# Pooled value rows inside block 0's value tiles, and a new order of the prologue: attention with pooled keys, then a gated MLP, on one core

## The chip, the core and the metric

The kernel runs on one core of a Trainium2 chip. The metric is the device time of one execution in microseconds (us). Three runs of the kernel before gave 698.35, 698.39 and 698.47, so its time is **698.39 us** (the median).

## What is computed

```python
def _attn_ref(q, k, v):                       # (4, 8, 768, 64) each, float32
    ...
    block, window = (32, 16)
    nb = S // block                           # 24
    k_sum = k.reshape(B, H, nb, block, D).max(axis=3)
    v_sum = v.reshape(B, H, nb, block, D).mean(axis=3)
    scores_l = scale * np.matmul(q, k.transpose(0, 1, 3, 2))
    mask_l = np.abs(pos[:, None] - pos[None, :]) < window
    scores_s = scale * np.einsum('bhsd,bhnd->bhsn', q, k_sum)
    scores_s = scores_s + np.log(block)
    ...  # masked scores_l and scores_s side by side, softmax over both: a
    v_all = np.concatenate([v, v_sum], axis=2)
    return np.matmul(a, v_all)

def _moe_ref(x, w_gate, w_val, w_out):        # x: the attention's output, 3072 x 512
    g = x @ w_gate                            # 512 x 1536
    silu = g * (1.0 / (1.0 + np.exp(-g)))
    return silu * (x @ w_val) @ w_out         # 1536 x 512
```

Every query thus sees 31 neighbouring keys and 24 pooled ones (a maximum over 32 keys for the scores, a mean over 32 rows for the values). The three weight matrices arrive as float64 and are turned into float32 on the chip.

## The kernel before

**Tiles.** The 3072 tokens are worked on as six blocks (k = 0 to 5) of 512. In a block the attention goes by head pairs (u = 0 to 3: two heads of 64 are the 128 partitions), the MLP by twelve weight tiles (j = 0 to 11, 128 of the 1536 hidden units each). 64 queries meet 96 keys at once (the window and its margins), and the 24 pooled keys stand behind them: a row of 120 scores (KC = 120, KW = 96).

**Steps of a head pair.** Scores on TensorE (`scores`; in block 0 apart as `sw` for the windows and `sp` for the pooled keys), row maxima on VectorE (`ttr0`, `ttr1`, L414), exponentials on ScalarE (`exp0`, `exp1`, L428), reciprocals of the sums on VectorE (`rcp`, L445 and L446), the scaling by them (`nrm`, L450), transposes on TensorE into PSUM (`tr0`, `tr1`, L465), their copies to SBUF (`pt0`, `pt1`, L162 or L164), the value products on TensorE (`out`, L492), and from PSUM the high and the low part of the result in the type fp32r (`split` makes xh, `rest` makes xl), which are the MLP's input. `zeros` (L598) issues filler matmuls on a tile of zeros; a digit behind a step's engine letter asks for so many columns of 128 of them ahead of the step.

**Steps of a weight tile.** A load on SyncE (`w_load`, raw_*), the magnitude on ScalarE (`w_abs`, L187, m_*), four integer steps on VectorE (`w_c1` L192, `w_c2` L196, `w_s1` L204, `w_s2` L211; the last two read two tensors), then the high part (`w_hi`, L162) and the low part (`w_lo`, L158) of w_*. g and v of tile 0 are handled apart, those of the other tiles together (gv); o is the output matrix. Then `gate` and `val` (L527: three products for each of four head pairs on 512 columns), `silu` (L533), `mul` (L538), `ah` and `al` (high and low part), and `down` (L577).

**The value tiles of block 0.** They lie in one SBUF tile, vrows, in three loads: vE (`ve`) the even value tiles and the matrix of means, vR (`vr`) the end of the even ones, vO (`vo`) the odd ones. `fv` (v_sums, L341) makes the block means of all values on TensorE, and `fvc` (v_keep) copies them to rows 96 to 119 of vs. For block 0 (OWN = (0,)) the value products contract over the 96 window rows alone (a_out, L492), and the 24 pooled rows are added by products of their own, `outp` (a_out_pooled, L500), two per head pair. In the later blocks a_values (L321 and the copy behind it) writes the pooled rows under the windows' values, and one product contracts over all 120 rows. A function v_copy that does the same for vrows (step `spc`) is there and unused.

**What sets the order.** The text PROLOGUE holds block 0's attention and MLP, block 1's attention, and the decoding of all weights. One word is one step; `=` and letters behind it choose its engine (a ScalarE, d VectorE, p GpSimd), its PSUM bank (g, y or c) and its fillers. The words are issued in the order of the text, and a chain of order dependencies (`after`) keeps that order on each engine, SyncE's queue of loads too. Behind it a loop runs blocks 1 to 5's MLP with the attention of blocks 2 to 5 put in at fixed places; the change leaves that loop alone. `after` takes no wait away: a step also waits for its data and for the buffers that it writes.

## Time and profile before

| | |
|---|---|
| median of three runs | 698.39 us |
| profiled execution, its own time | 698.23 us |
| span of its instructions | 696.4 us |
| TensorE (PE) busy | 687.0 us, 99% of the span, 4540 matmuls |
| weight loads (PEld), beside the matmuls | 558.0 us, 80% |
| VectorE (DVE) busy | 263.4 us, 38% |
| ScalarE (ACT) busy | 295.1 us, 42% |
| GpSimd (POOL) busy | 144.4 us, 21% |
| mean granted clock of TensorE | 0.999 of full speed |
| loads and stores over the span | 62.04 MB, 89 GB/s |

The span begins with the first instruction and ends with the last; the profiled execution's own time is 1.8 us longer. A share of busy time is a mean over the whole span: the page's 40 slices of 17.4 us show VectorE at six tenths or more in the first eight and at four or less in all later ones, and the transfers at seven tenths or more in the first five alone, while TensorE is at nine tenths or more from the third slice on, but for the last. A time in a row below is counted from the span's start.

### The profile page before, as it was taken

How to read it: one execution, taken by the hardware profiler on the slowest of the kernel's cores; microseconds unless marked ns; L12 is line 12 of the kernel's file. 1: busy time of each engine (PE TensorE's matmuls, PEld its weight loads, DVE VectorE, ACT ScalarE, POOL GpSimd, SP SyncE). 2: the span in 40 equal slices, each digit the busy share in tenths (PEclk: the TensorE clock that was granted, in tenths of full speed). 3: DMA queues.
4: the chain of work that ended last, by engine and by line, in shares of the span. 5: the costliest groups of instructions: out<-in, count | busy, mean ns of one | idle time of the engine just before them, and what ended most of it. 6: DMA issues, size and time to landing. Idle time of an engine off the chain costs nothing.

```text
span 696.4 us, 11370 instructions
## 1 busy us (share of the span) xinstructions
PE 687.0 (99%) x4540; PEld 558.0 (80%) x4540; DVE 263.4 (38%) x749; ACT 295.1 (42%) x707; POOL 144.4 (21%) x122
## 2 busy tenths in 40 slices
...
GB/s 341 325 323 294 274 72 133 85 155 118 84 62 0 62 56 88 84 26 58 107 24 144 74 56 61 3 60 61 61 62 53 8 24 1 61 1 0 1 0 61
DMA packets 52676, 62.04 MB, mean 89 GB/s; under 512 B 23152, under 2 KB 40944, under 8 KB 51088
## 3 DMA queue, kind: packets, MB, share of 16 engines
q1 hardware_dynamic: 52624, 61.32, 27.4%
q8 instruction: 36, 0.59, 0.4%
...
## 4 chain that ended last, share of the span: by engine, by line
PE 95%; DMA 3%; ACT 1%; DVE 0%; SPq 0%; issue 0%; DVEq 0%; ACTq 0%
PE g L527 29%; PE v L527 28%; PE acc L577 27%; PE xo L492 4%; PE sc L371 3%; PE pp L465 3%; DMA vrows<-in_vE 2%; DMA consts<-in_consts 1%; PE xo L500 1%; ACT p L428 0%; DVE w_gv L158 0%; DMA out<-o 0%; PE pp L598 0%; PE pv L341 0%; PE pv L320 0%; ACT L428 0%
## 5 line engine op out<-in xcount | busy, mean ns | idle before, releaser
L577 PE MATMUL acc<-w_o,ah 128*128 128x512 f32 x576 | 178.1, 390 | 0.0
L538 DVE TENSOR_TENSOR a<-v,a 128x512 f32<-128x512 f32 x72 | 49.6, 690 | 295.9 <-PE v L527 268.5
L527 PE MATMUL g<-xh,w_gv 128*128 128x512 f32 x480 | 160.3, 395 | 0.6 <-DVE w_gv L158 0.6
L527 PE MATMUL v<-xh,w_gv 128*128 128x512 f32 x480 | 158.2, 390 | 0.0
L158 POOL TENSOR_TENSOR al<-a,ah 128x512 fp32r<-128x512 f32 x63 | 81.5, 1294 | 322.0 <-ACT ah L162 322.0
L577 PEld LDWEIGHTS acc<-w_o,ah 128*128 128x128 f32 x576 | 108.2, 188 | 22.7
L577 PE MATMUL acc<-w_o,al 128*128 128x512 f32 x288 | 114.2, 397 | 0.0
L533 ACT ACTIVATE a<-g 128x512 f32<-128x512 f32 x72 | 43.1, 599 | 165.8 <-PE g L527 165.6
L527 PEld LDWEIGHTS g<-xh,w_gv 128*128 128x128 f32 x480 | 90.1, 188 | 23.0 <-issue 1.9
L527 PEld LDWEIGHTS v<-xh,w_gv 128*128 128x128 f32 x480 | 90.1, 188 | 18.8 <-issue 0.2
L162 ACT CAST ah<-a 128x512 fp32r<-128x512 f32 x72 | 44.7, 620 | 136.4 <-DVE a L538 136.3
L527 PE MATMUL g<-xl,w_gv 128*128 128x512 f32 x240 | 93.6, 390 | 0.0
L527 PE MATMUL v<-xl,w_gv 128*128 128x512 f32 x240 | 93.4, 389 | 0.0
L428 ACT ACTIVATE p<-p,nm 128x120 f32<-128x120 f32 x192 | 73.1, 382 | 5.7 <-DVE nm L414 5.5
L577 PEld LDWEIGHTS acc<-w_o,al 128*128 128x128 f32 x288 | 54.1, 188 | 10.8
L450 POOL TENSOR_TENSOR p<-p,ri 128x960 f32<-128x960 f32 x21 | 38.1, 1815 | 99.1 <-DVE ri L446 79.4
L527 PEld LDWEIGHTS v<-xl,w_gv 128*128 128x128 f32 x240 | 45.1, 188 | 9.2
L527 PEld LDWEIGHTS g<-xl,w_gv 128*128 128x128 f32 x240 | 45.1, 188 | 8.7
L414 DVE CUSTOM_DVE_ANT_0 p<-sc,consts 128x120 f32<-128x120 f32 x192 | 40.8, 277 | 3.5 <-PE sc L371 3.5
L428 ACT ACTIVATION_READ_ACCUMULATOR p<-p,nm 128x1 f32 x192 | 35.9, 187 | 0.0
L162 ACT CAST xh<-xo 128x512 fp32r<-128x512 f32 x24 | 13.9, 591 | 46.8 <-PE xo L492 46.8
L527 PE MATMUL g<-xh,w_g 128*128 128x512 f32 x96 | 32.9, 401 | 0.0
...
## 6 DMA issues: line engine op xcount, KB each, us to landing
raw_gv<-in_wgv SPq DMA_DIRECT2D x10, 1024.0 KB, 11.6
...
```

What stands on the lines that cost most here:

```text
L158: (nc.vector if e == "d" else nc.gpsimd).tensor_tensor(out=out, in0=a, in1=b.bitcast(F32), op=ALU.subtract)
L162: nc.scalar.copy(out, in_)
L371: nc.tensor.matmul(sc[h][s * QT : (s + 1) * QT, c * KC : (c + 1) * KC], t["q"][hs, qs], t["kw"][hs, i, :], start=True, stop=True,)
L414: nc.vector.tensor_tensor_reduce(out=t["p"][:, i, :], in0=t["sc"][g][:, c * KC : (c + 1) * KC], in1=bias_sb[:, 0 if n == 0 else 2 if n == ...
L428: nc.scalar.activation(out=t["p"][:, i, :], in_=t["p"][:, i, :], func=AF.Exp, scale=-1.0, bias=t["nm"][:, i : i + 1], accum_out=t["sm"][:, ...
L450: (nc.vector if on == "d" else nc.gpsimd).tensor_tensor(out=p, in0=p, in1=ri.rearrange("p (n o) -> p n o", o=1).broadcast_to([P, 2 * NTP, ...
L465: nc.tensor.transpose(ps[:KC, c * P : (c + 1) * P], U[k, u]["p"][:, g * NTP + c, :], id_sb)
L492: nc.tensor.matmul(ps[hs, qs], vw, t["pt"][:n, h, qs], start=k not in OWN or i == 0, stop=k not in OWN)
L527: nc.tensor.matmul(ps, w[:, cs], x, start=u == 0 and n == 0, stop=u == NP - 1 and n == 2)
L533: nc.scalar.activation(out=a, in_=A.pop(("g", k, j)), func=AF.Silu)
L538: nc.vector.tensor_tensor(out=a, in0=ps, in1=a, op=ALU.mult)
L577: nc.tensor.matmul(ACC[k][i], a[:, ts], w, start=j == 0 and n == 0, stop=j == NJ - 1 and n == 2)
```

## The change

OWN becomes empty, so block 0's value products contract over all 120 rows, as those of the other blocks. The pooled rows get into vrows by the step `spc` (v_copy), one copy of 24 partitions x 8 x 128 a head pair: pairs 1, 2 and 3 on ScalarE (`=a`), pair 0 on VectorE (`=d`). The step `outp` no longer stands in the table. The scaling `nrm` can run on ScalarE (`=a`) as eight multiplications of 128x120 by a factor per row; for pair 1 of block 0 (on VectorE before) and for all pairs of block 1 (on GpSimd, the last on VectorE) it does. Pairs 0 and 2 of block 0 stay on GpSimd, and pair 3 goes there from VectorE. The copies of pooled rows in block 1 (`values`) go from VectorE to ScalarE. The tile vs is made ahead of the table. Two further steps, kf and qf, are defined and not used, and a_out_pooled, no longer called, is written for the full height.

The table is in a new order throughout. In block 0's part the loads are issued in another order, and the fillers stand at other places (cc3, yc4, cy12, y3, g6, y4 and c9 in place of cy2, cg4, c2, g6, g8, y5 and g3). Behind it gate(0,3) now stands ahead of down(0,1), and in block 1 scores, transposes and value products stand at other places among the MLP's steps.

```diff
-OWN = (0,)
+OWN = ()
...
 PROLOGUE = """
...
-pt1(0,0)=a w_load(2,o) tr0(0,1)=g3 pt0(0,1)=a tr1(0,1)=c out(0,0)=c pt1(0,1)=a pt0(0,3)=a out(0,1)=y fvc()=a
-outp(0,1) outp(0,0) w_s2(1,o) w_hi(1,o)=a w_load(2,gv) w_c2(0,o) w_c1(1,gv) pt1(0,3)=a w_s2(0,v) w_s1(0,o)
...
+spc(3)=a spc(2)=a w_c1(0,o) rcp(0,1) w_hi(0,v)=d spc(0)=d w_load(1,o) w_c2(0,o) w_lo(0,v)=d out(0,0)=y4 spc(1)=a
+w_s1(0,g) w_s1(0,o) w_s2(0,g) w_s2(0,o) w_abs(1,gv) w_c1(1,gv) nrm(0,1)=a pt0(0,3)=a w_c2(1,gv) w_s1(1,gv)
...
 """
...
-            copy("d", U[k, u]["vw"][KW:, i : i + n], pooled(u).broadcast_to([NB, n, P]))
+            copy(on or "d", U[k, u]["vw"][KW:, i : i + n], pooled(u).broadcast_to([NB, n, P]))
...
     def v_keep():
 
-        vsum["all"] = one.tile([KC, DM], F32, tag="vs", name="vs_0")
...
     def a_scale(k, u):
         p, ri = U[k, u]["p"], U[k, u]["ri"]
+        if on == "a":
+            for i in range(2 * NTP):
+                nc.scalar.mul(p[:, i, :], p[:, i, :], ri[:, i : i + 1])
+            return
...
-            vw = vsum["all"][KW:, u * P + h * D : u * P + (h + 1) * D]
-            nc.tensor.matmul(t["xo"][hs, :TOK], vw, t["pt"][KW:, h, :], start=False, stop=True)
+            vw = vsum["all"][:, u * P + h * D : u * P + (h + 1) * D]
+            nc.tensor.matmul(t["xo"][hs, :TOK], vw, t["pt"][:, h, :], start=False, stop=True)
...
     pro = open_pool("pro")
     warm = pro.tile([P, DM], F32, name="warm")
     nc.vector.memset(warm, 0.0)
+    vsum["all"] = one.tile([KC, DM], F32, tag="vs", name="vs_0")
+    if 0 in OWN:
+        nc.gpsimd.memset(vsum["all"][:KW], 0.0)
```

**The first loads.** SyncE's queue up to the load of weight tile 1, in each. A name ends in its head pair (kq_2), block (kt_1), weight tile (raw_v0) or nothing of these (vrows), and a buffer number. Before:

```order
L251 DMA kq_2_93<-in_kq 128x1312
L251 DMA kq_0_131<-in_kq 128x1312
L611 DMA consts_135<-in_consts 128x488
L251 DMA kq_3_191<-in_kq 128x1312
L251 DMA kq_1_203<-in_kq 128x1312
L178 DMA raw_v0_205<-in_wgv 128x1024
L622 DMA vrows_226<-in_vR 32x512
L178 DMA raw_g0_260<-in_wgv 128x1024
L178 DMA raw_o1_297<-in_wo 128x1024
L178 DMA raw_o0_364<-in_wo 128x1024
L618 DMA vrows_226<-in_vE 128x3296
L178 DMA raw_gv1_408<-in_wgv 128x2048
```

With the change:

```order
L260 DMA kq_2_94<-in_kq 128x1312
L623 DMA consts_96<-in_consts 128x488
L260 DMA kq_0_118<-in_kq 128x1312
L260 DMA kq_3_169<-in_kq 128x1312
L178 DMA raw_v0_205<-in_wgv 128x1024
L260 DMA kq_1_207<-in_kq 128x1312
L178 DMA raw_g0_316<-in_wgv 128x1024
L178 DMA raw_o0_329<-in_wo 128x1024
L634 DMA vrows_331<-in_vR 32x512
L630 DMA vrows_331<-in_vE 128x3296
L638 DMA vrows_331<-in_vO 128x2048
L178 DMA raw_gv1_436<-in_wgv 128x2048
```

The constants come second, vO stands right behind vE, ahead of raw_gv1, and raw_o1 behind all of them; w_g0 and w_v0, the first weights that the MLP wants, keep the order v, g.

**From the block means to the first gate.** TensorE's queue behind `fv` (names end in block, pair and buffer number). Before, from `fv` on:

```order
L341 MATMUL pv_0_0_377<-vrows_226 32x128 x28
L598 MATMUL pp0_0_3_429<-warm_88 128x512
L598 MATMUL pp0_0_3_429<-warm_88 128x128
L465 MATMUL pp0_0_3_429<-consts_135,p_0_3_248 120x128 x4
L465 MATMUL pp1_0_3_436<-consts_135,p_0_3_248 120x128 x4
L598 MATMUL pp0_0_1_444<-warm_88 128x384
L465 MATMUL pp0_0_1_444<-consts_135,p_0_1_316 120x128 x4
L465 MATMUL pp1_0_1_452<-consts_135,p_0_1_316 120x128 x4
L492 MATMUL xo_0_0_457<-pt_0_0_413,vrows_226 64x64 x16
L492 MATMUL xo_0_1_477<-pt_0_1_450,vrows_226 64x64 x16
L500 MATMUL xo_0_1_477<-pt_0_1_450,vs_0_494 64x512 x2
L500 MATMUL xo_0_0_457<-pt_0_0_413,vs_0_494 64x512 x2
```

With the change, from `fv` to the last row ahead of the first gate (g_0_0):

```order
L350 MATMUL pv_0_0_387<-vrows_331 32x128 x28
L477 MATMUL pp0_0_3_422<-consts_96,p_0_3_252 120x128 x4
L477 MATMUL pp1_0_3_431<-consts_96,p_0_3_252 120x128 x4
L610 MATMUL xo_0_0_450<-warm_88 128x512
L504 MATMUL xo_0_0_450<-pt_0_0_384,vrows_331 64x64 x16
L504 MATMUL xo_0_2_492<-pt_0_2_418,vrows_331 64x64 x16
L610 MATMUL pp0_0_1_509<-warm_88 128x512 x2
L610 MATMUL pp0_0_1_509<-warm_88 128x128
L477 MATMUL pp0_0_1_509<-consts_96,p_0_1_341 120x128 x4
L477 MATMUL pp1_0_1_517<-consts_96,p_0_1_341 120x128 x4
L504 MATMUL xo_0_3_525<-pt_0_3_484,vrows_331 64x64 x16
L504 MATMUL xo_0_1_550<-pt_0_1_542,vrows_331 64x64 x16
```

The eight products of line 500 (two a pair) are gone. The value products (L492, now L504) of pair 3 and pair 1 are now the last rows ahead of the first gate; before, those of pairs 2 and 3 and their four pooled products were. The fillers (L598, now L610) have moved too.

**The chain that feeds them.** ScalarE's queue from the last copies ahead of the weights of tile 1 to the first xh. Before:

```order
L187 ACTIVATE m_gv1_422<-raw_gv1_408 128x1024
L162 CAST w_g0_427<-m_g0_262 128x512
L162 COPY pt_0_0_413<-pp1_0_0_367 120x512
L162 COPY pt_0_1_450<-pp0_0_1_444 120x512
L162 COPY pt_0_1_450<-pp1_0_1_452 120x512
L162 COPY pt_0_3_475<-pp0_0_3_429 120x512
L162 COPY vs_0_494<-pv_0_0_377 24x128 x4
L162 CAST w_o1_504<-m_o1_341 128x512
L162 COPY pt_0_3_475<-pp1_0_3_436 120x512
L187 ACTIVATE m_o2_550<-raw_o2_442 128x512
L162 CAST w_v0_552<-m_v0_287 128x512
L162 CAST xh_0_0_558<-xo_0_0_457 128x512
```

With the change, from the row behind the last exponentials of block 0:

```order
L162 COPY pt_0_2_418<-pp1_0_2_379 120x512
L162 COPY vs_0_90<-pv_0_0_387 24x128 x4
L162 COPY vrows_331<-vs_0_90 24x8x128 x3
L187 ACTIVATE m_gv1_473<-raw_gv1_436 128x1024
L460 ACTIVATE p_0_1_341<-p_0_1_341,ri_0_1_344 128x120 x8
L162 COPY pt_0_3_484<-pp0_0_3_422 120x512
L162 COPY pt_0_3_484<-pp1_0_3_431 120x512
L162 COPY pt_0_1_542<-pp0_0_1_509 120x512
L162 COPY pt_0_1_542<-pp1_0_1_517 120x512
L162 CAST w_gv1_548<-m_gv1_473 128x1024
L162 CAST xh_0_1_573<-xo_0_1_550 128x512
L162 CAST xh_0_2_583<-xo_0_2_492 128x512
```

Three copies into vrows (one row, x3) and the scaling of pair 1 (L460, x8) have come in; the casts of w_g0, w_v0 and w_o1 and the magnitude of o2 have left this stretch. VectorE's queue of the same stretch, behind its last maxima of block 0; before:

```order
L445 TENSOR_SCALAR sm_0_3_250<-sm_0_3_250 128x8
L446 RECIPROCAL ri_0_3_251<-sm_0_3_250 128x8
L196 TENSOR_SCALAR m_v0_287<-m_v0_287 128x512
L211 SCALAR_TENSOR_TENSOR m_g0_262<-raw_g0_260,m_g0_262 128x512
L204 SCALAR_TENSOR_TENSOR m_v0_287<-raw_v0_205,m_v0_287 128x512
L450 TENSOR_TENSOR p_0_3_248<-p_0_3_248,ri_0_3_251 128x960
L204 SCALAR_TENSOR_TENSOR m_o1_341<-raw_o1_297,m_o1_341 128x512
L445 TENSOR_SCALAR sm_0_1_318<-sm_0_1_318 128x8
L446 RECIPROCAL ri_0_1_319<-sm_0_1_318 128x8
L192 TENSOR_SCALAR m_o0_374<-m_o0_374 128x512
L450 TENSOR_TENSOR p_0_1_316<-p_0_1_316,ri_0_1_319 128x960
```

With the change:

```order
L453 TENSOR_SCALAR sm_0_3_254<-sm_0_3_254 128x8
L454 RECIPROCAL ri_0_3_255<-sm_0_3_254 128x8
L196 TENSOR_SCALAR m_g0_362<-m_g0_362 128x512
L164 COPY pt_0_0_384<-pp0_0_0_319 120x512
L164 COPY pt_0_0_384<-pp1_0_0_355 120x512
L164 COPY pt_0_2_418<-pp0_0_2_310 120x512
L211 SCALAR_TENSOR_TENSOR m_v0_264<-raw_v0_205,m_v0_264 128x512
L192 TENSOR_SCALAR m_o0_360<-m_o0_360 128x512
L453 TENSOR_SCALAR sm_0_1_343<-sm_0_1_343 128x8
L454 RECIPROCAL ri_0_1_344<-sm_0_1_343 128x8
L164 CAST w_v0_443<-m_v0_264 128x512
L164 COPY vrows_331<-vs_0_90 24x8x128
```

The scaling of pair 3 (L450) has gone to GpSimd, a step with one tensor stands behind each reciprocal (L454), and three copies of transposed tiles (L164) stand here in place of steps of w_o1.

## Rows read from the trace of the kernel before

**Rows 1.** Busy time of each engine in two stretches (start:end, length, then for PE, PEld, DVE, ACT and POOL the busy us and the number of instructions, the granted clock, the DMA share and GB/s).
```profile
20.00:25.00 5.00, 3.90 (x67) 2.66 (x67) 4.93 (x12) 5.00 (x19) 0.00 (x0) 1.00 1.00 413
...
200.00:400.00 200.00, 200.00 (x1335) 164.18 (x1330) 56.29 (x200) 80.67 (x205) 42.97 (x39) 1.00 0.24 68
```

**Rows 2.** Timeline of TensorE's matmuls from the arrival of the value rows to the first matmul on weight tile 1 (start us, us, engine, line, operation, out<-in, array tile, shapes, count; in brackets the idle time before it and what ended it).
```profile
21.47 1.87 PE L341 MATMUL pv<-vrows 128*32 128x128 f32 x56 [1.10 <-DMA vrows<-in_vE]
...
26.94 2.08 PE L492 MATMUL xo<-pt,vrows 96*64 96x64 f32 x64
28.95 1.93 PE L500 MATMUL xo<-pt,vs 24*64 24x512 f32 x8
...
32.83 1.93 PE L500 MATMUL xo<-pt,vs 24*64 24x512 f32 x8
34.69 0.50 PE L527 MATMUL g<-xh,w_g 128*128 128x512 f32 x1
...
40.34 0.39 PE L527 MATMUL g<-xh,w_gv 128*128 128x512 f32 x1
```

**Rows 3.** The chain of waits that ended last, in order of time (start us, us, what).
```profile
6.95 14.47 DMA vrows<-in_vE
```

**Rows 4.** Timeline of ScalarE in the prologue (columns as in rows 2).
```profile
14.61 0.68 ACT L187 ACTIVATE m_g<-raw_g 128x512 f32<-128x512 f32 x1 [0.96 <-DMA raw_g<-in_wgv]
...
21.98 0.38 ACT L428 ACTIVATE p<-p,nm 128x120 f32<-128x120 f32 x1
...
24.37 1.17 ACT L187 ACTIVATE m_gv<-raw_gv 128x1024 f32<-128x1024 f32 x1
...
25.94 2.23 ACT L162 COPY pt<-pp 120x512 f32<-120x512 f32 x4
28.18 1.07 ACT L162 COPY vs<-pv 24x128 f32<-24x128 f32 x4
...
33.04 1.06 ACT L162 CAST w_gv<-m_gv 128x1024 fp32r<-128x1024 f32 x1
```

**Rows 5.** Groups of instructions by line, each shape apart (line, engine, operation, out<-in and shapes, count; then busy us and the mean ns of one; then the idle time just before them and what ended it).
```profile
L414 DVE CUSTOM_DVE_ANT_0 p<-sc,consts 128x120 f32<-128x120 f32 x192 | 40.8, 277 | 3.5 <-PE sc L371 3.5
...
L287 DVE TENSOR_REDUCE ks<-kt 128x24 f32<-128x768 f32 x12 | 11.4, 948 | 3.4 <-DMA kt<-in_kP 3.4
...
L164 DVE COPY vw<-vs 24x1024 f32<-24x1024 f32 x12 | 8.3, 690 | 23.8 <-PE xo L492 23.6
...
L321 ACT ACTIVATE vs<-pv 24x128 f32<-24x128 f32 x12 | 3.2, 265 | 12.4 <-PE pv L320 10.9 <-DVE vw L164 1.4
```

**Rows 6.** Timeline of VectorE between its last maxima of block 0 and the first gate.
```profile
18.19 0.42 DVE L196 TENSOR_SCALAR m_g<-m_g 128x512 int32<-128x512 int32 x1
18.53 0.41 DVE L192 TENSOR_SCALAR m_v<-m_v 128x512 f32<-128x512 f32 x1
...
19.20 0.68 DVE L204 SCALAR_TENSOR_TENSOR m_g<-raw_g,m_g 128x512 int32<-128x512 int32 x1
19.80 0.41 DVE L196 TENSOR_SCALAR m_o<-m_o 128x512 int32<-128x512 int32 x1
...
29.85 1.22 DVE L204 SCALAR_TENSOR_TENSOR m_gv<-raw_gv,m_gv 128x1024 int32<-128x1024 int32 x1
```

**Rows 7.** Timeline of VectorE and of GpSimd, where both work on tiles in SBUF.
```profile
14.23 0.20 DVE L446 RECIPROCAL ri<-sm 128x8 f32<-128x8 f32 x1
15.32 1.33 DVE L192 TENSOR_SCALAR m_g<-m_g 128x512 f32<-128x512 f32 x1 [0.89 <-ACT m_g L187]
...
56.02 2.58 DVE L158 TENSOR_TENSOR w_gv<-m_gv,w_gv 128x1024 fp32r<-128x1024 f32 x1 [0.44 <-ACT w_gv L162]
...
14.58 1.79 POOL L450 TENSOR_TENSOR p<-p,ri 128x960 f32<-128x960 f32 x1 [0.96 <-DVE ri L446]
...
55.73 1.79 POOL L450 TENSOR_TENSOR p<-p,ri 128x960 f32<-128x960 f32 x1 [6.90 <-DVE ri L446]
```

**Rows 8.** Timeline of TensorE at three places where attention stands between MLP matmuls: for each the last MLP matmul ahead of the piece and the second behind it (those of x2 start 0.23 us apart); at the first place scores alone (line 371), at the second value products (line 492) and scores, at the third value products alone.
```profile
45.55 0.39 PE L527 MATMUL v<-xh,w_gv 128*128 128x512 f32 x1
...
47.19 0.40 PE L527 MATMUL g<-xl,w_gv 128*128 128x512 f32 x1
...
73.22 0.61 PE L577 MATMUL acc<-w_o,ah 128*128 128x512 f32 x2
73.77 1.15 PE L492 MATMUL xo<-pt,vw 120*64 120x64 f32 x32
...
76.17 0.39 PE L527 MATMUL g<-xl,w_gv 128*128 128x512 f32 x1
...
143.22 0.61 PE L577 MATMUL acc<-w_o,ah 128*128 128x512 f32 x2
...
145.19 0.63 PE L577 MATMUL acc<-w_o,ah 128*128 128x512 f32 x2
```

**Rows 9.** Weight tile 3: its load's issue on SyncE, the DMA issues of that moment and of the next weight tile (at 40.41) with KB and us from issue to landing, and TensorE's first matmul on tile 3.
```profile
37.74 0.43 SPq L178 DMA_DIRECT2D raw_gv<-in_wgv  x1
...
raw_gv<-in_wgv SPq DMA_DIRECT2D x1, 1024.0 KB, 9.2
...
raw_gv<-in_wgv SPq DMA_DIRECT2D x1, 1024.0 KB, 11.8
...
58.66 0.50 PE L527 MATMUL g<-xh,w_gv 128*128 128x512 f32 x1 [0.59 <-DVE w_gv L158]
```

More of the change, by code (lines that the diff above doesn't have):

```diff
@@ L116 @@
-gate(0,8) w_s1(8,o) rest(1,1) nrm(1,2)=p pool_values(1,2) tr0(1,2) pt0(1,2)=a load_values(1,2) mul(0,9)
-w_s2(10,gv) w_hi(10,gv)=a load(1,3) keys(1,3) values(1,2) val(0,8) w_s2(8,o) silu(0,8) w_hi(8,o)=a w_lo(8,o)=p
-tr1(1,2) w_lo(10,gv)=d mul(0,8) room(1) w_load(11,g) pt1(1,2)=a scores(1,3) out(1,2) w_abs(11,g) w_load(11,v)
-ah(0,8)=a w_load(11,o) ttr0(1,3) al(0,8)=d w_c1(9,o) ttr1(1,3) pool_values(1,3) w_c2(9,o) w_abs(11,v) w_c1(11,g)
-gate(0,10) w_s1(9,o) ah(0,9)=a w_c2(11,g) al(0,9)=p exp0(1,3) w_s2(9,o) w_s1(11,g) exp1(1,3) w_load(10,o)
@@ new lines @@
+w_s1(2,o) w_c2(5,gv) tr1(1,0) gate(0,4) w_s2(3,o) w_s2(2,o) mul(0,3) val(0,4) w_load(6,gv) w_s1(5,gv) pt0(1,0)=a
+w_load(4,o) al(0,2)=d ah(0,3)=a w_hi(2,o)=a load(1,1) w_load(7,gv) load_values(1,0) w_lo(2,o)=d w_abs(4,o)
+w_c1(4,o) w_s2(5,gv) w_load(9,gv) w_hi(3,o)=a w_hi(5,gv)=a down(0,2) silu(0,4) w_c2(4,o) w_abs(6,gv) keys(1,1)
+w_lo(5,gv)=d pt1(1,0)=a mul(0,4) w_c1(6,gv) ah(0,4)=a w_c2(6,gv) al(0,4)=p values(1,0)=a al(0,3)=p scores(1,1)
+gate(0,5) w_abs(7,gv) w_s1(4,o) pool_values(1,1) ttr0(1,1) ttr1(1,1) w_abs(9,gv) silu(0,5) w_s2(4,o) w_c1(9,gv)
@@ new lines @@
+exp1(1,1) w_hi(4,o)=a w_lo(3,o)=d w_c1(7,gv) w_s1(6,gv) w_load(7,o) w_load(6,o) w_load(5,o) w_c2(7,gv) exp0(1,1)
+out(1,0) split(1,0)=a w_lo(4,o)=d w_s2(6,gv) w_hi(6,gv)=a w_s1(7,gv) rcp(1,1) w_abs(5,o) nrm(1,1)=a w_abs(6,o)
+val(0,5) down(0,3) load(1,2) w_lo(6,gv)=d down(0,4) tr0(1,1) mul(0,5) w_c1(5,o) w_s2(7,gv) load_values(1,1)
+gate(0,6) w_c2(5,o) rest(1,0) w_hi(7,gv)=a tr1(1,1) w_c1(6,o) w_s1(5,o) w_abs(7,o) silu(0,6) pt0(1,1)=a
+pt1(1,1)=a w_s2(5,o) w_c1(7,o) w_lo(7,gv)=d keys(1,2) w_load(8,gv) ah(0,5)=a al(0,5)=p val(0,6) values(1,1)=a
```

82 lines of the change are left out of this document (42 added, 40 removed).

## The prediction, made before the changed kernel was run

> **What bounds the kernel now.** I read the busy time by windows first: from 200 to 400 us TensorE is busy for all of its 200 us, at a granted clock of 1.00, while VectorE and ScalarE work under half of that [rows 1]. There the time is a count of matmuls, and the change leaves that count alone. The total can move only by what happens ahead of it, so the sum below follows one mark: the moment when TensorE has done the same work in the same state.
>
> Then I read TensorE's timeline of the prologue. It waits for the value rows (vE) until 21.47 and then has no gap to 34.69, where block 0's first MLP matmul starts; the first matmul on weight tile 1 starts at 40.34 [rows 2]. Within that stretch the products on the pooled rows (line 500) start at 28.95 and 32.83 and take 1.93 each, the second up to the gate at 34.69: 1.86 without the overlap, 3.7 us in all. The chain of waits tells why it begins at 21.47: vE is issued at 6.95 and needs 14.47 us [rows 3]. Last I looked for stalls behind that: the one of note is 0.59 us before gate(0,3) at 58.66, which waits for VectorE's decoding of weight tile 3 [rows 9].
>
> **Removed and moved ahead of the first gate.** The eight pooled products go: 3.7 us off TensorE. The value products that remain contract over 120 rows in place of 96, with the same number of columns, and I charge nothing for that: the later blocks run them over 120, 1.15 us for 32 records [rows 8] against 2.08 for 64 [rows 2]. Each run has an end in it, so the difference is at most 0.1 a pass, 0.4 in all. But now every value product waits until the pooled rows stand in the value tiles, so the 3.7 us are only had if that chain is early.
>
> *The loads.* In front of vE one weight tile less is queued (raw_o1, 0.52 MB), at 413 GB/s [rows 1] that is 1.3 us: vE lands at 20.1 in place of 21.45. vO (1.05 MB) now comes right behind it, at 22.7, and then raw_gv1 (1.05 MB) at 25.2. The block means fv() take 1.87 [rows 2], so they end at 22.0.
>
> *ScalarE's chain.* Before, its last exponential of block 0 ended at 22.36. Its queue now has one weight tile less ahead of that (0.6) and the 0.96 us wait for raw_g goes, since raw_v is wanted first [rows 4]; against that, the last key tile lands later behind raw_v (0.52 MB, 1.3 us). I take 21.5; with one copy of a transposed tile (0.56) behind it ScalarE is free at 22.1, as fv() ends. From there the chain is: four copies of the sums, 1.07, to 23.2; three copies of 24x1024; the magnitude of tile 1, 1.17; eight scalings of 128x120; four copies of transposed tiles 2.23 [rows 4].
>
> The two new forms are not in the trace. A ScalarE copy of 24x1024: between 0.69 (VectorE's, the same shape) and 1.06 (ScalarE's 128x1024 cast) [rows 4, 5]; I take 1.03, since ScalarE's rows go by elements per partition. A scaling of 128x120 with a factor per row: between 0.265 (the 24x128 scaling) and 0.38 (the exponential's step, which has a sum to read out as well) [rows 4, 5]; I take 0.27. So: 23.2 + 3.1 = 26.3; + 1.1 (1.17 less the overlap) = 27.4; + 2.2 = 29.6; + 2.2 = 31.8. The last value product out(0,1) follows by half its length and ends at 32.9. **The first gate can start at 33.0**, against 34.69. With the upper price of the scalings it is 33.9, with the lower one of the copies 31.9.
>
> The Trainium skill, "ScalarE: Activation LUTs", section "What ACT_TABLE_LOAD costs", prices an ACTIVATE at 186 ns + 0.833 ns an element, 93 more for each per-row operand, and lets neighbours overlap by 93. By that, an estimate, a scaling is 0.286 us, and the sum below would end 0.1 later.
>
> *VectorE's chain.* It must have w_g0 ready by then. From start to start a fast step of 512 takes 0.34 (18.19 to 18.53), one with two tensors 0.60 (19.20 to 19.80), always some 0.08 less than its duration, so that one of 1024 takes 0.6 or 1.13 and a maximum 0.20 [rows 5, 6]. Its last maximum of block 0 ends near 17.2 (before 18.2 [rows 6]: the 0.89 idle and the 0.9 lost behind GpSimd go [rows 7], four maxima of another pair, 0.8, come in). To the high part of w_g0 and the last decoding step of tile 1 it then has 7 fast steps (2.4), 7 of 0.60 (4.2), three copies of transposed tiles (1.8), two reciprocals (0.7), its own pooled copy (0.69 [rows 5]), four steps of tile 1 (3.5), and a wait of about 0.6 for the sums: 17.2 + 13.9 = 31.1. GpSimd's low part (1.3) is ready at 32.4. So VectorE is second by 0.6 us.
>
> *To tile 1.* The 24 matmuls of tile 0 take 5.45 at 0.227 each; pair 1's high part follows out(0,1) on ScalarE (33.6) and its low part on VectorE (34.2), pairs 2 and 3 at 34.8 and 35.4, each as the interleaved order comes to it. The first matmul on tile 1 is at 38.4, against 40.34: **-1.9 us**. The 3.7 us of products are thus gone, yet 1.8 of them come back as waits for ScalarE, which eleven more filler matmuls of the idle slots cover (they cost nothing unless those waits vanish, then up to 11 x 0.21 us).
>
> **Behind it.** *Pieces between MLP matmuls.* A change from MLP matmuls to attention and back costs time: scores alone add 1.18 us, value products alone 1.28, both in one piece 2.26, so parting them costs 0.20 [rows 8]. In block 1's part the table goes from twelve pieces to sixteen: two partings of scores from values (0.20 each) and two of transposes (between 0 and 0.20; I take 0.10): **+0.6**.
>
> *Tile 3.* gate(0,3) now stands before down(0,1), so at the earlier start TensorE wants tile 3 at 38.4 + 5.45 (tile 1) + 2.72 (gate 2) + 1.2 (scores) + 5.44 = 53.2, against 58.66 - 0.59 = 58.07. raw_gv3 has no raw_o4 (0.52 MB, 1.3 us) in front of it now, and block 1's loads begin when block 0's value products end, at 32.9 in place of 34.7: it lands near 43.8 instead of 37.74 + 9.2 = 46.9 [rows 9]. From 35.4 VectorE's steps up to tile 3's low part are six of 1.13, five fast ones of 1024, five of 0.60, four of 0.34, two reductions of 0.87 [rows 5] and eight maxima, together 17.6, and I add 0.8 for casts and loads that it waits for: 53.8. The stall is 0.6, as before: **0**. What made it then goes: the scaling of block 1 ran on GpSimd, and VectorE's step of 1.22 took 2.58 beside it [rows 7]; ScalarE does that scaling now, 8 x 0.27 a pair. The eight copies of pooled rows that leave VectorE in block 1 make room for the casts and low parts that come to it, so I count nothing for either; that this cover may be short is a rival below.
>
> **Sum.** -1.9 + 0.6 + 0 = -1.3 us on the profiled execution's 698.23, so 696.9; the median of the runs, 698.39, lies 0.16 above that execution, so **697.1 us**. About what a measurement can tell from no change is 0.2%, or 1.4 us: the forecast lies on that edge.
>
> **The rivals.**
> *More is had.* The copies cost ScalarE 0.7 and tile 3 is in time: the gate is then held by w_g0 at 32.4, 0.6 sooner, and 0.4 of the stall goes: 696.1. For it: the lower end of the copy's price; against it: that end is another engine's row.
> *The decoding takes it back.* Counted on in the same way, VectorE has under 1 us in hand at tiles 6, 7 and 8; steps 1.1 us late there return what was won: 698.2. For it: so little slack. Against it: the copies of pooled rows, and the steps that waited for them, are gone.
> *GpSimd goes first.* VectorE's step beside a GpSimd product does not share, it waits: 2.58 for 1.22, ending at 58.60, 1.1 after GpSimd's end at 57.52 [rows 6, 7]. In the new order a fast step stands right behind each reciprocal that releases GpSimd. GpSimd began 0.15 us after the end of such a reciprocal (14.43 to 14.58 [rows 7]), so that step should be first. If not, VectorE loses 1.8 twice (0.6 of it was waiting), w_g0 is ready at 32.4 + 3.0 = 35.4 and tile 1 starts at 41.0, 0.7 after the old time; with +0.6 for the pieces, and 0.6 less for tile 3, which is then in time, it is 699.0. The Trainium skill, "GPSIMD Engine Reference", section "1. Specifications", says that its SBUF interfaces are shared with VectorE; by that rule the rival has its reason, and the rows agree (2.58 against 1.22).
> *Slower: tile 3 comes late.* If raw_gv3 still lands at 46.9, every step behind it on VectorE is 3.1 later, TensorE waits 3.7 at gate(0,3) instead of 0.6, and the time is 697.1 + 3.1 = 700.2. It decides from a landing at 45.1 (no gain) and 46.5 (slower by 0.2%). For it: the next load of its size needed 11.8 us [rows 9].
> *The change does not do what it says* would be value products that wait for vO as before; the order shows the loads moved, so I give it no chance of its own.
>
> **How the numbers follow.** Forecast 0.52, more 0.12, taken back 0.17, GpSimd first 0.07, tile 3 late 0.12. Faster by over 0.2% (below 697.0): just under half of the forecast's case, 0.25, the whole of "more", 0.12, and 0.05 of mixed cases: 0.42. Slower by over 0.2% (above 699.8): 0.12. The same: 0.46. The forecast's own range, from the bounds of the ScalarE prices and of the pieces, is 696.1 to 698.2. The range for 8 in 10 reaches to "more" with both prices low and to "GpSimd first": 695.8 to 699.3.
>
> **What would show it.** Right: no product of 24x512 on TensorE; vE landing near 20.1 and vO near 22.7; three ScalarE copies of about 1.03 and eight scalings near 0.27 in one row; the first gate near 33.0, the first matmul on tile 1 near 38.4, no TensorE wait above 0.7 us after it. Wrong: the gate held by VectorE or GpSimd, a wait for w_gv of over 1 us between 50 and 115 us, or a granted clock under 1.00 in the first 35 us.

## The result, and the profile after

The changed kernel takes **705.13 us** (median of 4 runs, 704.81 to 705.45) against 698.40 for the kernel before: a ratio of 1.0097, 95% interval [1.0083, 1.0110]. Foreseen were 697.1 us and a range of 695.8 to 699.3; the change is slower by 6.7 us.

The steady part is as before: from 200 to 400 us TensorE is busy for 200 us at a clock of 1.00 [rows 1]. Most of the loss stands between 110 and 140 us; no term of the prediction's sum reaches that far. Busy time by windows, changed kernel (columns as in rows 1):

```profile
120.00:130.00 10.00, 7.85 (x62) 6.02 (x60) 6.34 (x26) 3.42 (x4) 2.50 (x1) 1.00 0.50 150
130.00:140.00 10.00, 9.42 (x33) 7.17 (x34) 7.51 (x16) 9.85 (x29) 0.00 (x0) 0.83 0.16 49
...
200.00:400.00 200.00, 200.00 (x1293) 164.26 (x1292) 53.97 (x183) 78.20 (x194) 43.09 (x38) 1.00 0.22 64
```

TensorE's timeline of the changed kernel answers rows 2: the block means, the first value products, the first gate, the first matmul on tile 1, every wait of note behind it, and block 1's first MLP matmul.

```profile
20.94 1.87 PE L350 MATMUL pv<-vrows 128*32 128x128 f32 x56 [0.40 <-DMA vrows<-in_vE]
...
24.62 1.15 PE L504 MATMUL xo<-pt,vrows 120*64 120x64 f32 x32
...
33.56 0.50 PE L539 MATMUL g<-xh,w_g 128*128 128x512 f32 x1
...
39.11 0.39 PE L539 MATMUL g<-xh,w_gv 128*128 128x512 f32 x1
...
43.30 0.50 PE L539 MATMUL v<-xh,w_gv 128*128 128x512 f32 x1 [1.31 <-ACT a L545]
...
56.35 0.47 PE L539 MATMUL g<-xh,w_gv 128*128 128x512 f32 x1 [0.63 <-DVE w_gv L158]
...
114.04 0.47 PE L539 MATMUL g<-xh,w_gv 128*128 128x512 f32 x1 [0.40 <-DVE w_gv L158]
...
130.56 0.50 PE L539 MATMUL v<-xh,w_gv 128*128 128x512 f32 x1 [2.71 <-DVE a L550]
...
131.66 0.63 PE L539 MATMUL v<-xl,w_gv 128*128 128x512 f32 x1
132.09 1.05 PE L539 MATMUL v<-xh,w_gv 128*128 128x512 f32 x2
...
135.19 0.50 PE L589 MATMUL acc<-w_o,al 128*128 128x512 f32 x1
...
141.56 0.50 PE L539 MATMUL g<-xh,w_g 128*128 128x512 f32 x1 [0.19 <-DVE w_g L158]
...
154.56 0.40 PE L539 MATMUL g<-xh,w_g 128*128 128x512 f32 x1
```

In the kernel before, block 1's first MLP matmul is this row of the same view:

```profile
147.76 0.40 PE L527 MATMUL g<-xh,w_g 128*128 128x512 f32 x1
```

At that mark both kernels have done the same work, so the loss can be booked. The first row is part of the second, and the rows from the second on add up to the last:

| | before | changed | difference | foreseen |
|---|---|---|---|---|
| first gate | 34.69 | 33.56 | -1.1 | -1.7 |
| first matmul on tile 1 | 40.34 | 39.11 | -1.2 | -1.9 |
| waits from there to the mark | 0.59 | 5.24 | +4.7 | 0 |
| lower clock in val(0,10) | | 1.8 | +1.8 | 0 |
| rest, by subtraction (the sum had 0.6 for more pieces between MLP matmuls) | | | +1.6 | +0.6 |
| the mark | 147.76 | 154.56 | +6.8 | -1.3 |

The waits are 1.31, 0.63, 0.40, 2.71 and 0.19. Val(0,10) runs from 130.56 to 135.19, 4.63 us, against 2.83 in the first experiment below: its matmuls start 0.43 us apart (131.66 to 132.09) where others start 0.23 apart, and the granted clock is 0.50 from 131.5 to 134.8, which is the level of 1.2 GHz. It fell 0.9 us behind the end of the longest wait.

Where the longest wait comes from is read backwards. TensorE waits for mul(0,8) on VectorE. VectorE had been idle for 3.59 us before that, ahead of the first decoding step of tile 11:

```profile
128.92 0.43 DVE L192 TENSOR_SCALAR m_v<-m_v 128x512 f32<-128x512 f32 x1 [3.59 <-ACT m_v L187]
129.38 0.43 DVE L196 TENSOR_SCALAR m_v<-m_v 128x512 int32<-128x512 int32 x1
129.81 0.69 DVE L550 TENSOR_TENSOR a<-v,a 128x512 f32<-128x512 f32 x1
```

The chain of waits (start us, us, what) leads on from there:

```profile
120.28 1.06 ACT w_gv L162
121.34 0.07 issue
121.41 2.51 POOL w_gv L158
123.92 0.02 issue
123.94 4.27 DMA raw_v<-in_wgv
128.21 0.02 issue
128.23 0.66 ACT m_v L187
```

The load of raw_v11 is issued the moment GpSimd has the low part of tile 10. No step reads both tiles: the load waits for **memory**. The weights of tile 11 (`room(1)`) take the place of the three buffers in which weights are decoded (`dec`, tag m). The addresses in the built programs, in bytes of a partition, each tile 4096 bytes long:

```
         m_gv8   m_gv10   raw_g11  raw_v11  raw_o11
before   221152  225248   216448   220544   224640
changed  225248  221152   216448   220544   224640
```

Before, raw_v11 lies over all but the end of m_gv8; now over the same part of m_gv10, which is decoded last. No line of the diff says so. A new m takes the buffer that came free first in the order of the table: tile 4 was decoded ahead of tile 3 (m_gv4 at 225248, m_gv3 at 221152), now 3 comes ahead of 4 and the two addresses have changed places, and from there the two buffers are exchanged, down to tiles 8 and 10.

### The profile page after: what moved, and what is told of

It is laid out like the page before. It is cut to its first block, busy times and chain, and to the rows that moved or that the text cites. A ratio compares the mean times of both kernels' runs of the same rounds, so it can differ in the third digit from the quotient of the medians.

```text
span 703.0 us, 11417 instructions
## 1 busy us (share of the span) xinstructions
PE 689.4 (98%) x4544; PEld 557.9 (79%) x4544; DVE 264.5 (38%) x748; ACT 308.6 (44%) x747; POOL 142.8 (20%) x122
## 4 chain that ended last, share of the span: by engine, by line
PE 85%; DVE 4%; ACT 4%; DMA 4%; SPq 1%; issue 1%; POOL 0%; DVEq 0%; ACTq 0%
PE g L539 26%; PE acc L589 25%; PE v L539 25%; PE xo L504 3%; PE sc L379 3%; PE pp L477 2%; DMA vrows<-in_vE 2%; DVE m_gv L204 1%; DMA vt<-in_vT 1%; ACT p L460 1%; DMA raw_v<-in_wgv 1%; DVE m_gv L211 0%; ACT vrows L162 0%; DVE m_o L204 0%; ACT p L436 0%
## 5 line engine op out<-in xcount | busy, mean ns | idle before, releaser
L158 POOL TENSOR_TENSOR al<-a,ah 128x512 fp32r<-128x512 f32 x64 | 83.6, 1307 | 321.2 <-ACT ah L162 321.2
L462 POOL TENSOR_TENSOR p<-p,ri 128x960 f32<-128x960 f32 x19 | 34.0, 1792 | 76.3 <-DVE ri L454 65.0
L164 POOL COPY kw<-ks 128x96 f32<-128x96 f32 (+1 forms) x28 | 12.2, 437 | 108.4 <-DVE ks L296 65.5
```

The lines of the kernel that those rows point to most:

```text
L158: (nc.vector if e == "d" else nc.gpsimd).tensor_tensor(out=out, in0=a, in1=b.bitcast(F32), op=ALU.subtract)
L462: (nc.vector if on == "d" else nc.gpsimd).tensor_tensor(out=p, in0=p, in1=ri.rearrange("p (n o) -> p n o", o=1).broadcast_to([P, 2 * NTP, ...
```

## The experiments

All are made from one of the two kernels. A letter behind `=` is the engine, as in the table of steps.

**1. The buffers exchanged back.** Each m is given the buffer by name that it had in the changed kernel; the names get addresses in the order of first use, which exchanges two of the three: m_gv8 lies at 221152 again. Instructions and order stay.

```diff
+SLOT = {('v', 0): 'a', ('gv', 2): 'a', ('gv', 5): 'a', ('gv', 9): 'a', ('g', 0): 'c', ('gv', 3): 'c', ('gv', 6): 'c', ('gv', 8): 'c', ('gv', 1): 'b', ('gv', 4): 'b', ('gv', 7): 'b', ('gv', 10): 'b'}
...
-            m = dec.tile([P, len(nm) * DM], F32, tag="m", name=f"m_{nm}{j}")
+            m = dec.tile([P, 2 * DM], F32, tag=f"m{SLOT[nm, j]}", name=f"m_{nm}{j}")[:, : len(nm) * DM]
...
-    dec = open_pool("dec", 3, side="right")
+    dec = open_pool("dec", 1, side="right")
```

> The changed kernel with one thing exchanged: two of the three buffers in which weights are decoded swap addresses, so that raw_v of tile 11 is loaded over m_gv of tile 8 (done at 113.9) and no longer over m_gv of tile 10 (done at 123.9). No instruction and no order changes. Theory 1 (the load of tile 11 waits for a buffer): the load is issued near 114 in place of 123.94, VectorE's idle time of 3.59 at 128.92 and TensorE's wait of 2.71 at 130.56 go, and with them the lower granted clock behind that wait (1.8 us): about 700.5. Theory 2 (VectorE and ScalarE are simply late with the whole decoding, the load is only the last link): the wait moves to the next weight, less than 1.5 us is won: 703.7 or more.

Measured: **699.73 us** (699.19 to 700.55), ratio to the kernel before 1.0022 [1.0013, 1.0032]. 5.4 of the 6.7 us come back. SyncE issues the load at 113.75, 0.03 us after VectorE's low part of tile 8 ends, and val(0,10) starts without a wait:

```profile
113.75 0.33 SPq L179 DMA_DIRECT2D raw_v<-in_wgv  x1
```

```profile
127.43 0.48 PE L540 MATMUL v<-xh,w_gv 128*128 128x512 f32 x1
...
130.26 0.39 PE L590 MATMUL acc<-w_o,al 128*128 128x512 f32 x1
```

Theory 1 holds, with 0.8 us more than it foretold.

**2. The scalings of block 1 off ScalarE.**

```diff
-nrm(1,0)=a ... nrm(1,1)=a ... nrm(1,2)=a ... nrm(1,3)=a
+nrm(1,0)=p ... nrm(1,1)=p ... nrm(1,2)=p ... nrm(1,3)=d
```

> The changed kernel with the scalings of block 1 where they were before: pairs 0 to 2 on GpSimd, pair 3 on VectorE, in place of ScalarE (2.4 us each there). Theory 1 (the buffer of tile 11): ScalarE's chain to m_gv of tile 10 is up to 2.4 us shorter, so the buffer is free up to 2 us sooner and part of the wait goes, while VectorE loses about 1.2 us beside each GpSimd product: 702.5 to 705. Theory 2 (the scalings on ScalarE are the cause): nearly all comes back: 699 or less.

Measured: 710.82 us, ratio 1.0176 [1.0161, 1.0192]: slower by another 5.7, which neither theory had. TensorE waits for GpSimd itself now, for the pooled keys that stand behind a scaling in its queue and for scalings, 1.10 and 1.54 us:

```profile
75.11 1.05 PE L378 MATMUL sc<-kw,q 64*64 64x120 f32 x32 [1.10 <-POOL kw L163]
...
90.50 0.65 PE L476 MATMUL pp<-consts,p 128*120 128x128 f32 x4 [1.54 <-POOL p L461]
```

So the scalings on ScalarE are no cause of the loss; in this order they are needed.

**3 and 4. mul(0,0) early; low parts off GpSimd.** In the changed kernel mul(0,0), which frees the PSUM bank that val(0,1) writes, ends at 43.09 behind two other steps of VectorE. The row of the wait at 43.30 names a step of ScalarE that ended at 43.25; that mul(0,0) was it is shown by moving it: in experiment 3 val(0,1) starts without a wait at 42.48, ahead of that same step of ScalarE (43.82). Experiment 3 moves it; experiment 4 also puts two low parts on VectorE.

```diff
-... w_s2(2,gv) val(0,0,3) pool_values(1,0) w_hi(2,gv)=a mul(0,0) ...
+... val(0,0,3) mul(0,0) w_s2(2,gv) pool_values(1,0) w_hi(2,gv)=a ...
```

```diff
-w_lo(0,o)=p ... al(0,1)=p
+w_lo(0,o)=d ... al(0,1)=d
```

> The changed kernel with mul(0,0) (and the last piece of val(0,0) in the table) ahead of the last decoding step of tile 2 on VectorE, in place of behind that step and the reduction of block 1's first values. It ends near 41.0 in place of 43.1, so TensorE's wait of 1.31 at 43.30 goes. Theory 1 (the decoding of tile 3 pins TensorE): w_gv of tile 3 still comes at 56.2, the wait at gate(0,3) grows from 0.63 to about 1.9, and the total stays within 0.5 us of 705.1. Theory 2 (each wait is a loss of its own): 1.3 us less, 703.8.

> As the run with mul(0,0) early, and the low parts w_lo(0,o) and al(0,1) on VectorE in place of GpSimd. In the changed kernel VectorE's steps beside these two took 1.53 for 0.42 at 38.89 and 2.29 for 1.22 at 48.67. Theory 1 (GpSimd's products shut VectorE out, and tile 3 pins TensorE): VectorE has two steps of 0.6 more and 2.2 us of shut-out less, w_gv of tile 3 is ready about 1 us sooner, the wait at gate(0,3) is near 0.9 and the total about 1 us below that of the run with mul(0,0) early. Theory 2 (VectorE is bound by its number of steps): the wait at gate(0,3) grows by 1.2 and the total with it.

Measured: 704.04 us, ratio 1.0086 [1.0071, 1.0101], and 703.82, ratio 1.0082 [1.0067, 1.0097]. In experiment 3 the wait at 43.30 is gone and the one at gate(0,3) stays at 0.52, so theory 2 is right there, and for a reason that I had not thought of. VectorE and GpSimd at 48 us, in the changed kernel:

```profile
48.67 2.29 DVE L204 SCALAR_TENSOR_TENSOR m_gv<-raw_gv,m_gv 128x1024 int32<-128x1024 int32 x1
```

```profile
48.28 1.60 POOL L158 TENSOR_TENSOR al<-a,ah 128x512 fp32r<-128x512 f32 x1 [1.88 <-ACT ah L162]
```

and in experiment 3:

```profile
49.16 1.21 DVE L203 SCALAR_TENSOR_TENSOR m_gv<-raw_gv,m_gv 128x1024 int32<-128x1024 int32 x1
```

```profile
48.77 4.83 POOL L157 TENSOR_TENSOR al<-a,ah 128x512 fp32r<-128x512 f32 x1 [1.21 <-ACT ah L161]
```

The pair starts 0.39 us apart in both, but in the first VectorE stands still for 1.1 us, in the second GpSimd for 3.5. So w_gv of tile 3 came sooner of itself. Experiment 4 then had nothing to win at that place and is no judge of its theories; its wait at gate(0,3) is 1.27, in the slowest of its four executions.

**5. Experiments 1 and 3 together.**

> The changed kernel with the two decode buffers exchanged and mul(0,0) early, both at once. Theory 1 (the two losses lie in places that do not cover each other): the 1.1 us that mul(0,0) alone won comes on top of the 5.4 of the buffers: 698.6. Theory 2 (with tile 11 in time another weight takes the gain): 699.5 or more.

Measured: 699.14 us (698.26 to 700.60), ratio 1.0011 [1.0001, 1.0020]. In the profiled execution (698.35) the way from tile 1 to the mark is 108.7 us, against 110.0 in experiment 1, 115.45 in the changed kernel and 107.42 before. By the profile the 1.3 us are won, by the medians 0.6: between the theories, since its executions scatter (experiment 12).

**6. Products in place of copies.** Experiment 1 with OWN = (0,), the four `spc` steps left out and `outp(0,u)` behind each `out(0,u)`: the pooled products are back, in the new order.

```diff
-OWN = ()
+OWN = (0,)
...
-spc(3)=a spc(2)=a ... spc(0)=d ... out(0,0)=y4 spc(1)=a
+... out(0,0)=y4 outp(0,0)
```

> The changed order with the two decode buffers exchanged (699.73 without more), but with the pooled products in place of the pooled copies: each pair's two products stand right behind its value products, and the four copies into the value tiles are left out. TensorE gets 3.7 us of products, ScalarE loses 2.9 us ahead of the last value product and VectorE 0.7. Theory 1 (ScalarE's chain ends the prologue, the products would be paid in full): the last value product could come 2.9 us sooner, but TensorE with its fillers and 3.7 us more ends near 36.7 in place of 33.6, the first gate is up to 3 us later, and the total 700.7 to 702.8. Theory 2 (products and copies only change places, each 3 us on the path): the same within 0.5 us.

Measured: 700.92 us, ratio 1.0036 [1.0023, 1.0049], 1.2 above experiment 1. The first gate moves from 33.44 there to 34.92:

```profile
25.42 1.03 PE L512 MATMUL xo<-pt,vs 120*64 120x512 f32 x4
...
34.92 0.50 PE L539 MATMUL g<-xh,w_g 128*128 128x512 f32 x1
```

Theory 1, with half of its size: in this order the copies themselves are a gain, of 1.5 us at the first gate and 1.2 at the end.

**7. The new front, the old order behind it.** The table of the changed kernel up to val(0,0,3), mul(0,0), then what is left of the order before, in that order (a whole table; the 15 steps that it does late are named in the expectation).

> The new order up to the last piece of val(0,0), mul(0,0), and from there the order before, with all that it has left to do. At that point the new order has 15 steps undone that the order before had done by gate(0,1) (most of the decoding of the output weights 1 and 2 and the first step of tile 4, about 4.3 us of VectorE), and one done ahead (the last step of tile 2, 1.1). Theory 1 (the gain of the front is real, only the order behind it spoils it): the 1.2 us arrive at the end: 697.2. Theory 2 (the front is won by putting off 3 us of VectorE's decoding, and VectorE has no idle time until 110 us to make it good): TensorE waits for a weight between 50 and 115 us for 2 us or more, 699 or more.

Measured: 705.26 us, ratio 1.0106 [1.0089, 1.0123]. The first gate is at 33.62 as in the changed kernel; then the decoding put off stands ahead of block 1's pooled keys, whose reduction starts at 48.13 on VectorE against 44.74. TensorE waits for them, and the granted clock from 50 to 60 us is 0.71:

```profile
46.82 0.64 PE L378 MATMUL sc<-kw,q 64*64 64x120 f32 x14 [1.66 <-ACT a L544]
50.39 1.08 PE L378 MATMUL sc<-kw,q 64*64 64x120 f32 x16 [2.93 <-POOL kw L163]
52.06 0.79 PE L538 MATMUL g<-xh,w_gv 128*128 128x512 f32 x1 [0.60 <-DVE a L549]
```

By the time this is theory 2, but TensorE waits for the pooled keys and not for a weight. That part of the early gate is borrowed from VectorE fits this run; the lower clock and two waits of VectorE for ScalarE (0.74 and 0.93 us) have their share in it, and no run parts them.

**8. Copies in the old order.**

```diff
-ve() fv()=g8 w_load(1,gv) ... pt1(0,2)=a nrm(0,3)=d ... w_abs(1,gv) vo() ... out(0,1)=y fvc()=a
-outp(0,1) outp(0,0) ... outp(0,2) ... outp(0,3)
+ve() fv()=g8 vo() w_load(1,gv) ... pt1(0,2)=a fvc()=a spc(3)=a spc(2)=a spc(1)=a nrm(0,3)=d spc(0)=d ... w_abs(1,gv) ... out(0,1)=y
```

> The order before, with the pooled copies in place of the pooled products and little else: vO is loaded ahead of raw_gv of tile 1, the sums are copied to vs and into the value tiles (pairs 1 to 3 on ScalarE, pair 0 on VectorE) right behind the copies of pairs 0 and 2's transposed tiles. TensorE loses 3.7 us of products, ScalarE gets 2.9 us ahead of the copies of pairs 1 and 3's transposed tiles and raw_gv of tile 1 lands 2.5 us later. Theory 1 (ScalarE's chain takes back what TensorE wins): the first gate is at 34 to 36 against 34.69, and the total within 1.5 us of 698.4. Theory 2 (3.7 us of products on the path are 3.7 us): 695 to 696.

Measured: 703.70 us, ratio 1.0071 [1.0056, 1.0086]. The first gate is at 35.96, as theory 1 had it, but TensorE then waits 1.86 us for a low part of VectorE (xl), the clock from 30 to 40 us is 0.83, and tile 1 starts at 43.69 in place of 40.34. The total lies beyond both theories' figures: the wait for xl and the clock were in neither. At tile 1 this order is 3.4 us behind the kernel before; what makes the rest of the 5.3 is not shown. The copies are a gain in the new order (experiment 6) and a loss in this one.

**9. The buffers of the kernel before exchanged.** The edit of experiment 1 in the other kernel, where it brings m_gv10 under raw_v11.

> The kernel before, with the exchange of decode buffers the other way round: there raw_v of tile 11 is loaded over m_gv of tile 8, now over m_gv of tile 10. No instruction and no order changes. Theory 1 (this buffer alone makes the load late, in any order): the load cannot be issued before the low part of tile 10 ends, 122.1 in place of 116.91; it lands near 126.5, ScalarE stops 3 us for it at 123.35, and what stands behind it (exponentials, reciprocals and weight 11) comes 1 to 3 us later: TensorE waits, 699 to 701. Theory 2 (the order before has room there, the buffer only hurt because VectorE and ScalarE were late): within 0.3 us of 698.4.

Measured: 700.25 us (700.04 to 700.42), ratio 1.0024 [1.0015, 1.0033]: theory 1. ScalarE stands still for the load, 3.01 us, and TensorE later for 0.96:

```profile
126.61 0.68 ACT L188 ACTIVATE m_v<-raw_v 128x512 f32<-128x512 f32 x1 [3.01 <-DMA raw_v<-in_wgv]
```

```profile
132.91 0.47 PE L578 MATMUL acc<-w_o,al 128*128 128x512 f32 x1 [0.96 <-ACT w_o L163]
```

**10. Fillers in the long wait.** Their result is read by nothing.

```diff
                 nc.tensor.transpose(pv[:NB, :P], vsum[u], id_sb)
+                if (k, u) == (1, 3):
+                    for z in range(24):
+                        nc.tensor.matmul(pv[:, 256:], W["g", 10][0][:, :P], X[0, 0][0][:, :256], start=True, stop=True)
```

> The changed kernel with 24 matmuls of 256 columns, whose result nothing reads, ahead of val(0,10), where TensorE waits 2.71 us at 130.56; they take about 2.7 us. The wait for mul(0,8) stays. Theory 1 (TensorE's granted clock falls because it stood idle): the 12 matmuls behind run at the full clock again, 2.7 us in place of 4.6, and the total is 703.3. Theory 2 (the clock falls at that point for another reason): the clock is below 1 there as before, the total is 705.1 or more.

Measured: 704.83 us, ratio 1.0092 [1.0077, 1.0108]. The clock stays at 1.00 and the matmuls of val(0,10) start 0.23 us apart, so theory 1 is right about the clock; but 1.39 us of the gain are a new wait at the next step, for a low part (al) that the same late load holds up:

```profile
127.91 3.12 PE L332 MATMUL pv<-xh,w_gv 128*128 128x256 f32 x24
130.87 0.40 PE L542 MATMUL v<-xh,w_gv 128*128 128x512 f32 x1
...
135.16 0.50 PE L592 MATMUL acc<-w_o,al 128*128 128x512 f32 x1 [1.39 <-DVE al L158]
```

The step behind val(0,10) starts at 135.16 against 135.19, and the medians, 704.83 and 705.13, lie within each other's scatter. The 1.8 us of the lower clock were thus hardly a loss of their own: without them TensorE waits there.

**11. Two reductions moved as well.** Experiment 5 with `pool_values(1,0)` behind `w_lo(3,gv)` and `keys(1,3)` behind `w_lo(8,gv)`.

```diff
-... w_s2(2,gv) pool_values(1,0) ... w_lo(3,gv)=d ... keys(1,3) ... w_lo(8,gv)=d ...
+... w_s2(2,gv) ... w_lo(3,gv)=d pool_values(1,0) ... w_lo(8,gv)=d keys(1,3) ...
```

> The changed kernel with the two decode buffers exchanged, mul(0,0) early, and two reductions of VectorE (0.87 us each) put behind the low part for which TensorE waits: that of block 1's first values behind w_lo of tile 3, that of block 1's last keys behind w_lo of tile 8. Theory 1 (VectorE's queue sets when TensorE gets weights 3 and 8, waits of 0.48 and 0.42): both waits go, 698.2 by the median, and the fastest executions near 697.4. Theory 2 (the time is bound by VectorE's amount of work up to 113 us, whatever its order): the waits come back at another weight, 699.1.

Measured: 700.70 us, ratio 1.0034 [1.0021, 1.0046], slower than experiment 5 and than either theory. The wait for weight 8 is gone; the one at gate(0,3) is 1.76, and three of 0.27 to 0.44 are new. VectorE won 0.87 us by the move, lost 0.57 waiting for ScalarE in the gap, and lost 1.1 more because in this order its step stood still again beside al(0,1):

```profile
48.37 2.32 DVE L204 SCALAR_TENSOR_TENSOR m_gv<-raw_gv,m_gv 128x1024 int32<-128x1024 int32 x1
```

**12. Experiment 5 once more.**

> The kernel with buffers exchanged and mul(0,0) early once more, for a second profile of the same program. In its first profile GpSimd's al(0,1) started at 48.22 and took 4.84 us, while VectorE's step at 48.61 kept its 1.21; in the changed kernel and in the one with both reductions moved the same pair stood 0.39 us apart too, and GpSimd took 1.60 while VectorE's step took 2.3. Its ten timed executions lie between 698.3 and 700.6. Theory 1 (which engine waits differs from execution to execution, as the arrival of vE does): this profile shows another pair of durations, or another arrival of vE, and the time follows them. Theory 2 (the order of the program fixes both): the same durations within 0.1 us, vE at 21.0, and a time within 0.2 us of the first profile's 698.35.

Measured: 698.63 us, one execution. GpSimd's al(0,1) takes 4.84 us again and VectorE's step 1.21: in both profiles the order gives the same, theory 2. The block means start at 21.29 in place of 21.02, the first gate 0.30 later, and the time is 0.28 longer. Theory 1 would have vE arrive later, but vE was issued at 5.59, took 15.3 us and was there at 20.9, as in experiment 5 (5.49 and 15.48). TensorE itself was late: the last key tile landed at 14.03 (issued at 3.21, 10.82 us), VectorE's reduction of it starts at 14.06 in place of 13.02, and the transposes ahead of the block means wait for what hangs on it. The row of the block means names no wait for vE here, and one in experiment 5:

```profile
18.13 0.65 PE L477 MATMUL pp<-consts,p 128*120 128x128 f32 x4 [1.18 <-POOL p L462]
...
21.29 1.87 PE L350 MATMUL pv<-vrows 128*32 128x128 f32 x56
```

```profile
21.02 1.87 PE L350 MATMUL pv<-vrows 128*32 128x128 f32 x56 [0.70 <-DMA vrows<-in_vE]
```

So the arrival of a load did vary between two executions of one program, though it was another load than theory 1 named.

## Why the prediction was wrong

**What bounds the kernel: right in form.** The time did move by the shift of one mark, and behind it the kernels run alike (6.8 us at the mark, 6.6 in the span).

**To the first gate: right, 0.6 short.** The products of line 500 are gone, the three ScalarE copies took 1.04 us (1.03 foreseen), and the eight scalings 2.38 (2.2). ScalarE's chain of the changed kernel answers rows 4:

```profile
23.98 1.99 ACT L162 COPY vrows<-vs 24x1024 f32<-24x1024 f32 x2
25.87 1.04 ACT L162 COPY vrows<-vs 24x1024 f32<-24x1024 f32 x1
26.93 1.15 ACT L187 ACTIVATE m_gv<-raw_gv 128x1024 f32<-128x1024 f32 x1
27.98 2.38 ACT L460 ACTIVATE p<-p,ri 128x120 f32<-128x120 f32 x8
30.38 1.07 ACT L162 COPY pt<-pp 120x512 f32<-120x512 f32 x2
```

Start to start a scaling is 0.30 against my 0.27. The Trainium skill, "ScalarE: Activation LUTs", section "What ACT_TABLE_LOAD costs", gave an estimate of 0.286, which is nearer. The larger miss is vE, 20.9 in place of 20.1. I took its load to gain all of the time of raw_o1, which was moved behind it, at 413 GB/s. By the windows of the two traces 0.6 MB less had indeed moved when vE landed (7.0 against 7.6 MB), but at a mean of 335 GB/s in place of 355, and vE needed 15.00 us from issue against 14.47 [rows 3]. Why the rate was lower is not shown. The row that answers rows 3:

```profile
5.90 15.00 DMA vrows<-in_vE
```

With this the gate came at 33.56 for 33.0.

**Pieces: right in kind, too small.** Four more partings were put at 0.6. Experiment 5, freed of the two large losses, needs 1.3 us more than before from tile 1 to the mark, of which 0.3 are waits (0.48 and 0.42 against 0.59). The 1.0 that remain are put down to the pieces by subtraction; no run has the pieces alone.

**Tile 3: the wait was 0.63 as forecast (0.6), but by luck: two errors cancel.** VectorE had w_gv of tile 3 2.4 us later than counted. The prediction said of the shut-out by GpSimd's scaling "What made it then goes"; it went, and two low parts on GpSimd did the same, 1.53 for 0.42 at 38.89 and 2.29 for 1.22 at 48.67. TensorE too came late, since it waited 1.31 us for mul(0,0), which the new order puts behind two other steps. The prediction had asked when VectorE ends the weights, and never when it frees the banks; by experiment 3 that wait cost 1.1 us. (VectorE's steps up to tile 3 add up to 17.5 and not 17.6, and the rival "GpSimd goes first" has tile 1 at 40.9 and not 41.0; neither changes a reading.)

**What failed.** The step that failed is the last term, "**0**": it covers tile 3's wait, and for all that lies behind tile 3 the sum has nothing. VectorE's steps were counted on up to tile 8, and what could be lost there was entered as the rival "The decoding takes it back", at 698.2. Two things were left out. The count stopped two tiles short of the end of decoding, and it asked for engines alone: that a load must find its buffer free stood in no term, although the document ahead of the prediction says that a step waits for the buffers that it writes. The order of VectorE's steps changed which buffer tile 10 sits in, so raw_v11 was issued at 123.94 in place of 116.91; experiment 1 gives 5.4 us of the loss of 6.7 to this, and experiment 9 shows the same buffer costing 1.9 us in the old order. With mul(0,0) moved as well (experiment 5) 6.0 come back. The mark was well chosen; the way to it was not walked to its end.

**The rivals.** None was it. "GpSimd goes first" did not come true where it was priced (a step of VectorE was first behind each reciprocal), but its mechanism struck at two other places. "Tile 3 late" had the right kind, a load that comes late, at the wrong tile. "More" failed at the gate.

**What would show it.** vE near 20.1 and no wait above 0.7 us were named as signs, and both speak against the forecast: 20.9, and waits of 1.31 and 2.71. The sign named for the decoding, a wait for w_gv above 1 us between 50 and 115 us, did not appear; the large one came at 130.

None of the versions beats the kernel before: the best, experiment 5, is at 1.0011 [1.0001, 1.0020] of it. Its gain of 1.1 us at tile 1 is more than spent by the mark: 0.3 on waits and 1.0 on the rest, which I put down to the pieces.
